# Two-row-block transfers for half-height output weights, a V half in five pieces, and a ring of 14 units between layers in a two-layer decode block

## The chip, the cores and the metric

The kernel runs on one core of one Trainium2 chip. The metric is device time in microseconds (us) of one launch, here the time of one core. TensorE (PE) multiplies matrices, VectorE (DVE), ScalarE (ACT) and GpSimd (POOL) do the element-wise work, and the queue of SyncE (SP) issues nearly all transfers from HBM to on-chip memory. Sixteen DMA engines carry them out.

## The reference

Four blocks follow each other on two rows `x` of 512 numbers (batch 2, one token): attention, feed-forward, attention, feed-forward, each with a layer norm in front and added to `x`.

```python
def _A_ref(x, k_cache, v_cache, wq, wo):       # 32 query heads, 8 KV heads, 32768 cached tokens, Dh 128
    q = (x @ wq).reshape(B, Sq, Hq, Dh).transpose(0, 2, 1, 3)
    k = jnp.repeat(k_cache, 4, axis=1); v = jnp.repeat(v_cache, 4, axis=1)
    p = _softmax(jnp.einsum("bhqd,bhkd->bhqk", q, k) * (Dh ** -0.5), axis=-1)
    o = jnp.einsum("bhqk,bhkd->bhqd", p, v)
    return o.transpose(0, 2, 1, 3).reshape(B, Sq, Hq * Dh) @ wo
def _B_ref(x, w_gate, w_up, w_down):           # 512 -> 1792 -> 512
    return (_gelu(x @ w_gate) * (x @ w_up)) @ w_down
x = x + _A_ref(_layernorm(x), ...); x = x + _B_ref(_layernorm(x), ...)
x = x + _A_ref(_layernorm(x), ...); x = x + _B_ref(_layernorm(x), ...)
```

Both layers read the same caches and weights. All is float32.

## The kernel before, in words

Everything streamed lies in one tile `M` of 110 *units*. A unit is 128 partitions by 512 numbers, 2 KB a partition and 0.262 MB in all. Units 0 to 31, 32 to 63 and 64 to 95 are the slots A, B and C. A head (KV head g, batch row b) needs four slot loads: K in two halves and V in two halves of 32 units each. The slots are used in turn. Units 96 to 107 are a zone of three places of four units (`PL = [96, 100, 104]`), for output weights while heads run and for the smaller matrices between the layers. Units 106 to 109 also hold the softmax's probabilities and its transposes.

All transfers stand in one list, `plan`, made by `add`, `chunk`, `stream` and `add_wo` before the program is written. `pump` issues from its head as long as the target units are free. `free(u, n)` marks units free after the instructions that read them and calls `pump`. The order of transfers is thus fixed, and each waits in SP's queue for the readers of its units. Eight completion semaphores (`DMAHW0` to `DMAHW7` in the listings) are handed out in rotation, so a transfer also waits for the one that stands eight before it.

Output weights: for KV head g, four units (`wo`), multiplied in `project` after the second batch row of g. For g = 3 all four, and for g = 5 two of them, are kept in half height instead (`WIDE = {3: 4, 5: 2}`, array `wl`): each unit becomes two of 64 partitions. `pump` brings them in by eight transfers of eight rows, every fourth row of a block of 32:

```python
for r in (0, 32):
    for j in range(4):
        nc.sync.dma_start(mem(u, n)[r + j:r + 32:4], src[r + j:r + 32:4])
```

That is 1 MB for g = 3 and 0.5 MB for g = 5, in each layer.

A head: `scores` (64 unit products, L304), `softmax`, `values` (64 unit products, L348), `combine`, and after the second batch row `project`. A feed-forward: `center` (mean and residual, L257 to L268), `products` (gate and up weights `gu`, 28 units, L403), `gelu`, `hidden`, `down` (`wd`, 14 units, L446). At the start of an attention layer `center`, then 32 units of `wq` (`query_unit`, L277), `query_copy`, `query_gather`.

Layer 1 walks the heads in reverse, so that its first head is layer 0's last. Of that head 101 of 128 units are kept on chip: all of V, the second half of K (32 units, slot C), and five units of the first half of K, which are copied into free PSUM banks and back. Between the layers `gu`, `wd` and `wq` stream through the three places in turn, four units each. Layer 0's last V half comes in pieces of 24, 4 and 4 units, as does layer 1's. In layer 1's feed-forward `gu` and `wd` go to the slots C and A, `wd` in pieces of 8, 2, 2, 1 and 1; the last `wd` unit is multiplied in another form (L466) after the sum `W` has been copied out.

A copy of a whole bank is made in two halves, `halves` and `scaled`, by ACT and by DVE, and `center` sums its row in two halves as well.

Of the kernel before, what the change touches and what calls it, by code (L numbers as in the profile page):

```python
# [11 lines left out]
F32 = mybir.dt.float32  # L12
# [23 lines left out]
PL = [96, 100, 104]  # L36
# [8 lines left out]
KFREE = CH - NPS  # L45

# [26 lines left out]
def block_kernel(ctx: ExitStack, tc: tile.TileContext, x, consts, kt, vt, wq, wo, wl, gu, wd, out):  # L73
# [13 lines left out]
    sm = cp.tile([P, 24], F32, name="sm")  # L87
# [4 lines left out]
    linv, sq2, rs, var = sm[:, 6:10], sm[:, 10:12], sm[:, 12:14], sm[:, 14:15]  # L92
    rstd, junk, nscale, half, ones = sm[:, 15:16], sm[:, 16:20], sm[:, 20:21], sm[:, 21:22], sm[:, 22:23]
# [11 lines left out]
    def pump():  # L105
        while plan:
# [7 lines left out]
            if src.shape[0] == P:  # L114
                nc.sync.dma_start(mem(u, n), src)
            else:
                for r in (0, 32):
                    for j in range(4):
                        nc.sync.dma_start(mem(u, n)[r + j:r + 32:4], src[r + j:r + 32:4])
# [50 lines left out]

    def add_wo(l, g):
# [7 lines left out]
    for l in range(2):  # L179
# [4 lines left out]
        else:  # L184
            ring = [SLOT_A, SLOT_B, SLOT_C]
            g, b = orders[1][0]
            add(("wq7",), cols(wq, 28, 4), PL[1], 4)
            stream("wq", 1, wq, 28, (4,) * 7, [PL[0], PL[2], PL[1], PL[0], PL[2], PL[1], PL[0]])
            where = {}
            lo = 0  # L190
            for n, u in [(4, PL[2])] + [(4, SLOT_C + 4 * i) for i in range(5)] + [(KFREE - 24, PL[0])]:
                key = ("k", 1, g, b, 0, lo)
                add(key, cols(kt[b, g, 0], lo, n), u, n)
                for i in range(n):
                    where[lo + i] = (key, u + i)
                lo += n
            pieces[("k", 1, g, b, 0)] = where
            g, b = orders[1][1]
            chunk("k", 1, g, b, 0, SLOT_C, (12, 20), 20)
# [5 lines left out]
        for i, (g, b, nm_, h) in enumerate(todo):  # L205
# [33 lines left out]
    zero = xw[:, 0, 0:1].to_broadcast([P, U // 2])  # L239
# [11 lines left out]
    def halves(dst, src):  # L251
        nc.scalar.copy(dst[:, :U // 2], src[:, :U // 2])  # L252
        nc.vector.tensor_copy(dst[:, U // 2:], src[:, U // 2:])  # L253

    def center():
        ws = mem(U_PT + 1)
        nc.scalar.activation(ws[:, :U // 2], W[:, :U // 2], AF.Copy, accum_out=rs[:, 0:1])  # L257
# [3 lines left out]
        for j in range(2):  # L261
            nc.tensor.matmul(X[:, :KC * 4], rs[:, j:j + 1].to_broadcast([P, P]), neg, start=False, stop=(j == 1))
# [17 lines left out]
    def scaled(dst, src):  # L280
        nc.scalar.activation(dst[:, :U // 2], src[:, :U // 2], AF.Copy, scale=rstd)
        nc.vector.tensor_scalar(dst[:, U // 2:], src[:, U // 2:], rstd, None, op0=OP.mult)
# [72 lines left out]
    def combine(acc, oT, g, b):  # L355
        md = mem(U_PT)
        halves(md, acc)
# [279 lines left out]
```

## Time and profile before

| | us |
|---|---|
| three runs | 2602.56, 2600.39, 2602.66 (median 2602.56) |
| the profiled execution: time | 2601.85 |
| its span, first to last instruction | 2600.0 |
| PE busy / weight loads / DVE / ACT in it | 1396.8 / 416.4 / 147.7 / 73.2 |
| HBM read | 1102.93 MB, 424 GB/s over the span |
| mean granted TensorE clock | 0.731 |

The busy times are those of the span. A row of the windows' table gives, for a stretch, each engine's busy time with its count of instructions in brackets, then the granted clock of TensorE, the mean busy share of the 16 DMA engines, and GB/s. Packets are put to the stretch in which they start, so a share can read over 1 in a short stretch. In the chain of work and in the timeline a row has the start, the duration, the engine and the line.

### The profile page before, as it was taken

Reading aid. Unit: us, or ns where it says so; the run is one execution under the profiler, and the core shown is the slowest. Engines: PE = TensorE matmul, PEld = TensorE weight load, DVE = VectorE, ACT = ScalarE, POOL = GpSimd, SP = SyncE. Lnnn points to the kernel's source line nnn. Section 1 sums busy time; section 2 is a strip of 40 time slices with the busy share of each in tenths; the row PEclk is TensorE's granted clock in tenths of the full one; section 3 lists DMA queues with packets and bytes.
Section 4 is the critical chain, followed back from the end, with each engine's and each line's share of the span. In section 5 each row is a group of like instructions: output and inputs, shape, how many; then the busy total and the mean of one; then the engine's idle time right before and its main releaser. Section 6 shows DMA issues by size and latency. Waiting matters only on the chain.

```text
span 2600.0 us, 20521 instructions
## 1 busy us (share of the span) xinstructions
PE 1396.8 (54%) x9558; PEld 416.4 (16%) x9558; DVE 147.7 (6%) x437; ACT 73.2 (3%) x196; POOL 3.2 (0%) x12
## 2 busy tenths in 40 slices
PE   4544554554555545555576455455545464554556
PEld 1111111111111111111122111111111111111112
DVE  0000000000000000000011000000000000000001
ACT  0000000000000000000000000000000000000000
POOL 0000000000000000000000000000000000000000
PEclk9777776677767777776788777667777677776677
DMA  9999999999999999999999999999999999999998
GB/s 421 433 434 434 429 432 434 432 436 410 429 429 435 434 397 435 433 429 435 410 340 431 440 432 434 433 395 434 433 427 435 411 435 435 431 433 433 433 430 352
DMA packets 27092, 1104.25 MB, mean 425 GB/s; under 512 B 3456, under 2 KB 3584, under 8 KB 4608
## 3 DMA queue, kind: packets, MB, share of 16 engines
q1 hardware_dynamic: 26720, 1102.86, 98.7%
q8 instruction: 75, 1.23, 0.2%
q10 hardware_dynamic: 288, 0.09, 0.0%
q14 instruction: 9, 0.07, 0.0%
HBM read 1102.93 MB, written 0.00 MB: 424 GB/s over the span
## 4 chain that ended last, share of the span: by engine, by line
DMA 67%; PE 22%; another core or an unknown queue 10%; issue 0%; DVE 0%; SPq 0%; ACT 0%; ACTq 0%; DVEq 0%
DMA M<-in_vt 51%; PE bank L348 14%; DMA M<-in_kt 13%; PE bank L304 5%; DMA M<-in_wd 1%; DMA cst<-in_consts 1%; PE bank L277 1%; PE bank L446 0%; PE bank L384 0%; PE bank L360 0%; DMA M<-in_gu 0%; PE bank L403 0%; DMA M<-in_wq 0%; PE bank L260 0%
## 5 line engine op out<-in xcount | busy, mean ns | idle before, releaser
L304 PE MATMUL bank<-M,qw 128*32 128x512 f32 x4096 | 588.3, 733 | 515.7 <-DMA M<-in_kt 515.7
L348 PE MATMUL bank<-M 128*16 128x512 f32 x4096 | 583.1, 733 | 482.8 <-DMA M<-in_vt 482.8
L304 PEld LDWEIGHTS bank<-M,qw 128*32 128x32 f32 x4096 | 143.1, 131 | 952.0 <-DMA M<-in_kt 564.9
L348 PEld LDWEIGHTS bank<-M 128*16 128x16 f32 x4096 | 137.4, 113 | 901.5 <-issue 901.4
L307 DVE TENSOR_REDUCE sm<-bank 128x1 f32<-128x512 f32 x64 | 44.3, 692 | 1105.6 <-PE bank L304 1105.6
L332 PE MATMUL bank<-cst,M 128*128 128x128 f32 x256 | 51.1, 348 | 90.5 <-ACT M L329 90.3
L329 ACT ACTIVATE M<-bank,sm 128x512 f32<-128x512 f32 x64 | 43.4, 683 | 1284.4 <-DVE sm L324 1284.4
L253 DVE COPY M<-bank 128x256 f32<-128x256 f32 x33 | 14.0, 425 | 1071.5 <-ACT M L252 1071.5
L332 PEld LDWEIGHTS bank<-cst,M 128*128 128x128 f32 x256 | 36.9, 176 | 100.9 <-ACT M L329 100.9
L333 DVE COPY M<-bank 128x512 f32<-128x512 f32 x64 | 43.8, 692 | 62.7 <-PE bank L332 62.7
L360 PE MATMUL bank<-cst,M 128*128 128x4 f32 x224 | 29.5, 255 | 26.7 <-DVE M L253 26.7
L252 ACT COPY M<-bank 128x256 f32<-128x256 f32 x33 | 12.3, 372 | 1120.4 <-PE bank L348 1112.4
L360 PEld LDWEIGHTS bank<-cst,M 128*128 128x128 f32 x224 | 27.1, 191 | 52.4 <-DVE M L253 52.4
L323 PE MATMUL bank<-cst,sm 128*128 128x128 f32 x32 | 10.3, 322 | 35.0 <-DVE sm L322 35.0
L403 PE MATMUL bank<-M,xw 128*32 128x512 f32 x112 | 22.1, 761 | 5.7 <-DMA M<-in_gu 3.3
L337 PEld LDWEIGHTS bank<-cst,sm 128*128 128x128 f32 x128 | 23.1, 253 | 0.0
L384 PE MATMUL bank<-M,oT 128*2 128x512 f32 x104 | 20.7, 806 | 3.0 <-DVE oT L362 3.0
L277 PE MATMUL bank<-M,xw 128*32 128x512 f32 x128 | 20.8, 746 | 1.8 <-DMA M<-in_wq 1.0
L337 PE MATMUL bank<-cst,sm 128*128 128x4 f32 x128 | 21.1, 270 | 0.0
L248 PE MATMUL bank<-cst,xin 128*2 128x128 f32 x40 | 6.0, 300 | 23.3 <-DMA cst<-in_consts 23.3
L446 PE MATMUL bank<-M,hT 128*2 128x512 f32 x54 | 12.2, 859 | 5.6 <-DMA M<-in_wd 3.7
L323 PEld LDWEIGHTS bank<-cst,sm 128*128 128x128 f32 x32 | 4.2, 133 | 64.4 <-DVE sm L322 64.4
(75 smaller groups left out, 179.8 us busy)
## 6 DMA issues: line engine op xcount, KB each, us to landing
M<-in_wo SPq DMA_DIRECT2D x12, 1024.0 KB
M<-in_vt SPq DMA_DIRECT2D x2, 6144.0 KB
M<-in_wq SPq DMA_DIRECT2D x2, 4096.0 KB
M<-in_gu SPq DMA_DIRECT2D x8, 1024.0 KB
M<-in_wq SPq DMA_DIRECT2D x8, 1024.0 KB
M<-in_kt SPq DMA_DIRECT2D x2, 4096.0 KB
M<-in_kt SPq DMA_DIRECT2D x6, 1024.0 KB
M<-in_gu SPq DMA_DIRECT2D x3, 2048.0 KB
```

The costliest lines, as they stand in the source:

```text
L277: nc.tensor.matmul(Q[32 * k:32 * k + 32, :], xw[:, k, XO - 2 * g:XO - 2 * g + 32], mem(u), start=start, stop=stop)
L304: nc.tensor.matmul(S[32 * t:32 * t + 32, :], w[:, 28 - 4 * c:60 - 4 * c], mem(u), start=start, stop=stop)
L307: nc.vector.tensor_reduce(mx[:, h:h + 1], S, axis=AX.X, op=OP.max)
L323: nc.tensor.transpose(X[:, :P], nm.to_broadcast([P, P]), ident)
L329: nc.scalar.activation(p[h], S[h], AF.Exp, bias=bias, scale=SCALE, accum_out=ls[:, h:h + 1])
L332: nc.tensor.transpose(S[h][:, k * P:(k + 1) * P], p[h][:, k * P:(k + 1) * P], ident)
L333: nc.vector.tensor_copy(mem(U_PT + h), S[h])
L337: nc.tensor.matmul(X[:, P:P + REP], ls[:, h:h + 1].to_broadcast([P, P]), mask, start=(h == 0), stop=(h == 1))
L348: nc.tensor.matmul(acc[32 * t:32 * t + 16, :], mem(U_PT + h)[:, k * P + 32 * t + 16 * e:k * P + 32 * t + 16 * e + 16], mem(u), start=(h == ...
L360: nc.tensor.matmul(X[:, :REP], md[:, c * P:(c + 1) * P], sel[:, 4 * c:4 * c + 4], start=(c == 2), stop=(c == 1))
L384: nc.tensor.matmul(W[32 * t:32 * t + NB, :], oT[:, t, :], mem(u + t - nw), start=(t > 0 and first), stop=final)
L403: nc.tensor.matmul(G[v][32 * t:32 * t + 32, :], xw[:, k, XO:XO + 32], mem(un), start=(k == 0), stop=(k == KC - 1))
```

## The change

Four edits, which go together in one file:

1. The half-height weights are stored with rows in another order, and each block of 32 rows comes in one transfer. The eight rows `j` of the old transfer number `j` are now the middle index of a three-dimensional source, with eight as its outermost size.
2. The zone gets a fourth place of two units, 94 and 95, the last two units of slot C, so that the ring between the layers has 14 units. For it only 30 units of K's second half are kept, 99 units in all, and its last two are loaded again (`k1`). The order in the ring is 104, 94, 96, 100, with 4, 2, 4 and 4 units; the first head's scores follow it.
3. The last V half of each layer comes in pieces of 8, 8, 8, 4 and 4 units, and layer 1's `wd` in 4, 4, 2, 2, 1 and 1.
4. `halves` and `scaled` go: ACT alone copies the bank (512 columns), `center` sums with one ACT instruction and one matmul for the mean instead of two, and the layer norm's scale is applied in `query_gather`, from `rstd2` (two columns), rather than in the copy. `feedforward` makes its one-column `rstd` from it by one more DVE instruction.

```diff
-PL = [96, 100, 104]
+PL = [96, 100, 104, 94]
+RING = [2, 3, 0, 1]
+SIZE = [4, 4, 4, 2]
+KC1 = 30
...
                 for r in (0, 32):
-                    for j in range(4):
-                        nc.sync.dma_start(mem(u, n)[r + j:r + 32:4], src[r + j:r + 32:4])
+                    nc.sync.dma_start(mem(u, n)[r:r + 32], src[r:r + 32].rearrange("(j i) c -> i j c", j=4))
...
+    def ring_stream(name, l, src, total, at):
+        cuts, places, n = [], [], 0
+        while n < total:
+            p = RING[at % 4]
+            cuts.append(SIZE[p])
+            places.append(PL[p])
+            n += SIZE[p]
+            at += 1
+        stream(name, l, src, total, cuts, places)
...
-            add(("wq7",), cols(wq, 28, 4), PL[1], 4)
-            stream("wq", 1, wq, 28, (4,) * 7, [PL[0], PL[2], PL[1], PL[0], PL[2], PL[1], PL[0]])
-            for n, u in [(4, PL[2])] + [(4, SLOT_C + 4 * i) for i in range(5)] + [(KFREE - 24, PL[0])]:
...
+            add(("wq7",), cols(wq, 28, 4), PL[2], 4)
+            ring_stream("wq", 1, wq, 28, 1)
+            stream("k0", 1, kt[b, g, 0], KFREE, (2, 6, 4, 4, 4, 4, 3),
+                   [PL[3]] + [SLOT_C + i for i in (0, 6, 10, 14, 18)] + [PL[1] + 1])
+            add(("k1",), cols(kt[b, g, 1], KC1, CH - KC1), PL[2], CH - KC1)
             g, b = orders[1][1]
-            chunk("k", 1, g, b, 0, SLOT_C, (12, 20), 20)
+            chunk("k", 1, g, b, 0, SLOT_C, (10, 22), 22)
...
-            chunk(nm_, l, g, b, h, ring[i % 3], (24, 4, 4) if last else (CH,))
+            chunk(nm_, l, g, b, h, ring[i % 3], (8, 8, 8, 4, 4) if last else (CH,))
...
-            stream("gu", 0, gu, 28, (4,) * 7, [PL[0], PL[2], PL[1], PL[0], PL[2], PL[1], PL[0]])
-            stream("wd", 0, wd, 14, (4, 4, 4, 2), [PL[2], PL[1], PL[0], PL[2]])
+            ring_stream("gu", 0, gu, 28, 0)
+            ring_stream("wd", 0, wd, 14, 0)
...
-            stream("wd", 1, wd, 14, (8, 2, 2, 1, 1), [SLOT_A, SLOT_A + 8, SLOT_A + 10, SLOT_A + 12, SLOT_A + 13])
+            stream("wd", 1, wd, 14, (4, 4, 2, 2, 1, 1), [SLOT_A + i for i in (0, 4, 8, 10, 12, 13)])
...
-        nc.scalar.activation(ws[:, :U // 2], W[:, :U // 2], AF.Copy, accum_out=rs[:, 0:1])
-        nc.vector.tensor_tensor_reduce(ws[:, U // 2:], W[:, U // 2:], zero, 1.0, 0.0, OP.add, OP.add, rs[:, 1:2])
+        nc.scalar.activation(ws, W, AF.Copy, accum_out=rs)
...
-        nc.vector.tensor_tensor_reduce(junk[:, :NB], v, par, 1.0, EPS, OP.mult, OP.add, var)
-        nc.gpsimd.tensor_tensor(rstd, var, half, op=OP.pow)
+        nc.vector.tensor_scalar_add(var, v, EPS)
+        nc.gpsimd.tensor_tensor(rstd2, var, half.to_broadcast([P, NB]), op=OP.pow)
...
     def query_copy(Q, dst):
-        scaled(dst, Q)
+        nc.scalar.copy(dst, Q)
...
-        nc.vector.tensor_copy(qT[:, :, lo:lo + n, :],
-                              G[:, :REP * 2 * n].rearrange("p (r g b) -> p r g b", r=REP, b=NB))
+        nc.vector.tensor_tensor(qT[:, :, lo:lo + n, :],
+                                G[:, :REP * 2 * n].rearrange("p (r g b) -> p r g b", r=REP, b=NB),
+                                rstd2.unsqueeze(1).unsqueeze(1).to_broadcast([P, REP, n, NB]), op=OP.mult)
...
-        halves(md, acc)
+        nc.scalar.copy(md, acc)
...
+    early = [0, 4, 4, 4, 3, 4, 4, KC1]
+    for m in range(8):
+        n = SIZE[RING[(m + 1) % 4]]
+        u = at(where[s][0])
+        for j in range(n):
+            query_unit(X, s // 4, s % 4, u + j, s < 4, s >= 24)
+            s += 1
+        free(u, n)
...
+        for j in range(min(early[m], KC1 - i)):
             score_unit(S1, w, i, k1[i][1], i < 4, i >= CH - 4)
             free(k1[i][1])
             i += 1
...
+    u = at(("k1",))
+    for i in range(KC1, CH):
+        score_unit(S1, w, i, u + i - KC1, False, True)
+        free(u + i - KC1)
+    peak(S1, 1)
     peak(S0, 0)
```

How the change moves instructions is seen on SP's queue at two places. The listings below give each transfer's line, its target and source tile, its shape (partitions by numbers), how often it stands in a row, and in brackets the semaphores that it waits for; `PE_49`, `DVE_49` and `Activation_49` stand for readers of the target units.

The first place is the middle of layer 0, at the output weights of KV head 3. Before, on SP:

```order
L115 DMA M<-in_vt 128x16384 [waits DMAHW5_49,DMAHW2_49,PE_49]
L119 DMA M<-in_wl 8x4096 [waits DVE_49]
L119 DMA M<-in_wl 8x4096 x4
L119 DMA M<-in_wl 8x4096 [waits DMAHW3_49]
L119 DMA M<-in_wl 8x4096 [waits DMAHW4_49]
L119 DMA M<-in_wl 8x4096 [waits DMAHW5_49]
L115 DMA M<-in_vt 128x16384 [waits DMAHW6_49,PE_49]
```

Now, at the same place:

```order
L119 DMA M<-in_vt 128x16384 [waits DMAHW5_49,DMAHW2_49,PE_49]
L122 DMA M<-in_wl 32x1x4096 x2
L119 DMA M<-in_vt 128x16384 [waits DMAHW3_49,PE_49]
L119 DMA M<-in_kt 128x16384 [waits DMAHW4_49,PE_49]
L119 DMA M<-in_kt 128x16384 [waits DMAHW5_49,PE_49]
```

Before, the last three of the eight small transfers wait for the three slot loads ahead of them, the eighth for the V half right in front (`DMAHW5`), and the next V half stands behind it. Now neither small transfer waits, and the V half behind them waits for readers and for a transfer eight places back.

The second place is between the layers, from the last output weights (`wo`) on. Before, on SP:

```order
L115 DMA M<-in_wo 128x2048
L115 DMA M<-in_gu 128x2048
L115 DMA M<-in_gu 128x2048 [waits PE_49]
L115 DMA M<-in_gu 128x2048 [waits DMAHW7_49,DMAHW4_49,PE_49]
L115 DMA M<-in_gu 128x2048 [waits DMAHW5_49,DMAHW0_49,PE_49]
L115 DMA M<-in_gu 128x2048 [waits DMAHW6_49,DMAHW1_49,PE_49]
L115 DMA M<-in_gu 128x2048 [waits DMAHW7_49,DMAHW2_49,PE_49]
L115 DMA M<-in_gu 128x2048 [waits DMAHW3_49,DMAHW0_49,PE_49]
L115 DMA M<-in_wd 128x2048 [waits DMAHW1_49,PE_49]
```

Now, from the same transfer on:

```order
L119 DMA M<-in_wo 128x2048
L119 DMA M<-in_gu 128x2048 [waits DMAHW3_49,PE_49]
L119 DMA M<-in_gu 128x1024 [waits DMAHW4_49]
L119 DMA M<-in_gu 128x2048 [waits DMAHW5_49]
L119 DMA M<-in_gu 128x2048 [waits DMAHW6_49,DMAHW2_49,PE_49]
L119 DMA M<-in_gu 128x2048 [waits DMAHW7_49,DMAHW3_49,PE_49]
L119 DMA M<-in_gu 128x1024 [waits DMAHW4_49,DMAHW0_49,PE_49]
L119 DMA M<-in_gu 128x2048 [waits DMAHW5_49,DMAHW1_49,PE_49]
L119 DMA M<-in_gu 128x2048 [waits DMAHW6_49,PE_49]
L119 DMA M<-in_wd 128x2048 [waits DMAHW7_49,PE_49]
```

Before, two `gu` pieces (8 units) stand ahead of the one that waits for `project` to release the last `wo` (the third); now three pieces of 10 units do, and the fourth waits for it.

More of the change, by code (lines that the diff above doesn't have):

```diff
@@ L460, in feedforward @@
             ws = mem(U_PT + 1)
-            halves(ws, W)
+            nc.scalar.copy(ws, W)
             for n in range(FD - tail, FD):
@@ L501, in block_kernel @@
             k0 = pieces[("k", 0, g, b, 0)]
+            free(SLOT_C + KC1, CH - KC1)
             free(k0[0][1], KFREE)
@@ L551, in block_kernel @@
             i += 1
-        if gg == 5:
-            take(PL[1], 4)
-            for q, (m, dst) in enumerate([(30, PL[1]), (31, PL[1] + 1), (27, PL[1] + 2), (28, PL[1] + 3)]):
-                (nc.scalar.copy if q % 2 else nc.vector.tensor_copy)(mem(dst), bank[psum[m]])
-    peak(S1, 1)
+        if m == 5:
+            take(PL[0], 4)
+            for q, kk in enumerate((30, 31, 27, 28)):
+                (nc.scalar.copy if q % 2 else nc.vector.tensor_copy)(mem(PL[0] + q), bank[psum[kk]])
+        if m == 6:
+            take(PL[1], 1)
+            nc.vector.tensor_copy(mem(PL[1]), bank[psum[29]])
     restart()
@@ L560, in block_kernel @@
     wnext = window(*orders[1][1])
-    take(PL[0] + 3, 1)
-    nc.scalar.copy(mem(PL[0] + 3), bank[psum[29]])
-    S0, A1 = bank[0], bank[1]
-    where = pieces[("k", 1, g, b, 0)]
-    held = {30: PL[1], 31: PL[1] + 1, 27: PL[1] + 2, 28: PL[1] + 3, 29: PL[0] + 3}
+    where = pieces[("k0", 1)]
+    held = {30: PL[0], 31: PL[0] + 1, 27: PL[0] + 2, 28: PL[0] + 3, 29: PL[1]}
     seq = list(range(24)) + [30, 31, 27, 28, 29] + [24, 25, 26]
-    seen, left = {}, {}
-    for i in seq:
-        left[i % 4] = i
+    left = {i % 4: i for i in seq}
+    seen = set()
     for i in seq:
```

49 lines of the change are left out of this document (13 added, 36 removed).

## The prediction

> **What bounds the kernel now.** First the page's slices and the shares of the chain of waits:
>
> ```profile
> GB/s 421 433 434 434 429 432 434 432 436 410 429 429 435 434 397 435 433 429 435 410 340 431 440 432 434 433 395 434 433 427 435 411 435 435 431 433 433 433 430 352
> DMA 67%; PE 22%; another core or an unknown queue 10%; issue 0%; DVE 0%; SPq 0%; ACT 0%; ACTq 0%; DVEq 0%
> ```
>
> Transfers bound it: nearly every slice of 65 us moves 430 to 435 GB/s, whatever PE does. What can be won lies in the slices that fall short: 410, 397, 395 and 411 (numbers 10, 15, 27, 32), 340 in the middle, 352 at the end. So I asked for windows around these (after the last engine's busy time: granted clock, DMA share, GB/s):
>
> ```profile
> 610.00:650.00 40.00, 19.49 (x141) 6.56 (x141) 2.72 (x8) 1.45 (x4) 0.00 (x0) 0.71 0.95 405
> 930.00:970.00 40.00, 18.82 (x141) 6.51 (x141) 2.63 (x8) 1.45 (x4) 0.00 (x0) 0.74 0.90 377
> 1290.00:1400.00 110.00, 88.91 (x609) 29.68 (x605) 14.12 (x52) 8.69 (x23) 1.41 (x3) 0.85 0.93 370
> 1730.00:1770.00 40.00, 18.43 (x137) 6.23 (x129) 2.72 (x8) 1.45 (x4) 0.00 (x0) 0.76 0.90 379
> 2040.00:2080.00 40.00, 15.57 (x93) 5.59 (x97) 2.72 (x8) 1.45 (x4) 0.00 (x0) 0.59 0.92 389
> 2080.00:2540.00 460.00, 243.85 (x1690) 69.67 (x1682) 23.87 (x65) 10.92 (x30) 0.00 (x0) 0.73 1.00 433
> ```
>
> The undisturbed pace is 433 GB/s, so a unit of 0.262 MB takes 0.605 us. A window of length t at r GB/s has lost t x (433 - r) / 433: 2.6, 5.2, 5.0 and 4.1 us at the four short places, 16.9 together, and 16.0 us between the layers.
>
> **Edit 1, the half-height weights.** The four short places are those of `wl`. Their cause stands in SP's waits and its timeline:
>
> ```profile
> SPq L119 <- DMA M<-in_kt: 103.8, 8, 20.3
> SPq L119 <- DMA M<-in_vt: 74.8, 4, 18.7
> 584.66 50.84 SPq L119 DMA_DIRECT2D M<-in_wl  x8
> 635.61 0.37 SPq L115 DMA_DIRECT2D M<-in_vt  x1
> ```
>
> Eight small issues hold SP's queue for 50.84 us: the last three, in each of four places, wait for slot loads that run (12 waits), since the completion semaphores go round by eight. The next V half is issued only at 635.61, after the load ahead has landed, so no slot load is queued behind it. With two transfers the listing shows neither wait; the V half behind them then needs only its slot, which PE releases long before. These stops go, and 24 issues with them; what is late next is the engines themselves. How they run in the stop shows in windows of 1 us, two of the place with 1 MB and four of one with 0.5 MB:
>
> ```profile
> 632.00:633.00 1.00, 0.00 (x0) 0.00 (x0) 0.00 (x0) 0.00 (x0) 0.00 (x0) 0.50 0.43 180
> 633.00:634.00 1.00, 0.00 (x0) 0.00 (x0) 0.00 (x0) 0.00 (x0) 0.00 (x0) 0.50 0.51 213
> 1748.00:1749.00 1.00, 0.00 (x0) 0.00 (x0) 0.00 (x0) 0.00 (x0) 0.00 (x0) 0.50 0.02 8
> 1749.00:1750.00 1.00, 0.00 (x0) 0.00 (x0) 0.00 (x0) 0.00 (x0) 0.00 (x0) 0.50 0.39 94
> 1750.00:1751.00 1.00, 0.00 (x0) 0.00 (x0) 0.30 (x2) 0.00 (x0) 0.00 (x0) 0.50 0.77 229
> 1751.00:1752.00 1.00, 0.07 (x1) 0.07 (x2) 0.00 (x1) 0.90 (x3) 0.00 (x0) 0.50 1.46 446
> ```
>
> At 1 MB about half the rate is left: `wl` goes to eight of the sixteen engines, and these have work through the stop while the others stand. At 0.5 MB all stand for about 1.8 us (0.98 + 0.61 + 0.23). A slot load has landed only when its last engine is done, and the eight have more bytes: 1.57 MB a layer over eight engines of 433 / 16 GB/s is 7.3 us. Low end: only what the eight lose returns, 2 x 1.8 = 3.6 us. High end: with all else equal the other eight end up 14.5 us ahead, half of it idle on the mean, so 16.9 - 7.3 = 9.6 us. I take 5.5, nearer the low end, because the last engine decides.
>
> Whether 32 rows stay on eight engines no row shows, since the old form had eight rows. [...]
>
> **Edits 2 and 3, between the layers.** The chain of waits there, with SP's release of the last place and three windows:
>
> ```profile
> 1288.54 8.85 PE bank L348 x64
> 1297.47 0.38 ACT M L252
> 1300.77 0.48 ACT M L257 x2
> 1303.13 0.89 PE bank L262 x4
> 1304.26 1.94 PE bank L403 x8
> 1309.87 7.06 DMA M<-in_gu
> 1332.20 0.48 ACT M L257 x2
> 1336.31 1.94 PE bank L277 x8
> 1300.77 11.94 SPq L115 DMA_DIRECT2D M<-in_gu  x5
> 1300.00:1305.00 5.00, 3.68 (x24) 2.33 (x20) 0.95 (x7) 0.64 (x3) 0.00 (x0) 0.74 0.64 211
> 1305.00:1310.00 5.00, 4.80 (x26) 1.09 (x18) 0.17 (x2) 0.00 (x0) 0.55 (x1) 0.58 0.56 185
> 1335.00:1340.00 5.00, 4.74 (x23) 1.85 (x23) 0.68 (x7) 0.45 (x2) 0.55 (x1) 0.51 0.74 269
> ```
>
> PE starts on V's last half at 1288.54, when the 24-unit piece has landed; the other eight units land 8 x 0.605 = 4.8 us later, at 1293.4, but PE ends at 1297.39. In pieces of eight it keeps pace (8.85 / 4 = 2.2 us for each, against 4.8 to load one), and after the landing has four units, 8 of 64 instructions: 1.1 us by this row, 1.9 by L403's eight. So values end near 1294.9, 2.5 us earlier. With edit 4 (below, 0.8 us) the last place is released at about 1297.7 rather than 1300.77, and the first `gu` place at 1302.9 rather than 1306.20.
>
> Meanwhile the queue held, behind V, `wo` and two `gu` pieces: 12 units, 7.3 us, spent at 1300.7. Then came one piece, then nothing until 1306.20: the windows lost 2.6 and 2.9 us. Now 14 units last until 1301.9, and the piece released at 1297.7 until 1304.3, when the next can start: up to 1 us is lost, 4.5 are saved. From the last `wd` (1332.2) to the first use of `wq` (1336.31 + 1.94) nothing is released for 6.1 us; the window lost 1.9. A chain 0.8 us shorter and two units more (1.2 us) cover that. Of the other 16.0 - 5.5 - 1.9 = 8.6 us, gaps behind single pieces, a ring that starts full should save most; I say 7.3. Against this stand two units more to load, 1.2 us. Edit 2 and 3 here: 4.5 + 1.9 + 7.3 - 1.2 = 12.5 us. Low end: the ring changes nothing and the chain alone does, 3.3 - 1.2 = 2.1; high end 16.0 - 1.2 = 14.8. I take 12.5, since each of the two gaps is filled by its own account. The first head's two peaks now follow each other, 0.7 us on DVE, behind the last loaded K units; the slot that this releases is wanted only after 32 further units (19 us of loading), which covers it.
>
> **Edit 4, the copies.** ACT's copy of a whole bank is in the trace, and so is the old pair:
>
> ```profile
> 1357.03 0.58 ACT L562 COPY M<-bank 128x512 f32<-128x512 f32 x1
> 2595.34 0.37 ACT L252 COPY M<-bank 128x256 f32<-128x256 f32 x1 [8.03 <-PE bank L446]
> 2595.81 0.42 DVE L253 COPY M<-bank 128x256 f32<-128x256 f32 x1 [4.14 <-ACT M L252]
> ```
>
> The halves ran one after the other, 0.89 us from start to end, since DVE waited for ACT; one copy saves 0.3. `center` saves 0.1 on its sum and half of L262's 0.89 us: 0.8 together, counted above. In the heads the same saving hides behind transfers, as do the added DVE instruction and the scale in the gather.
>
> **The tail.** Here everything after the last transfer counts:
>
> ```profile
> 2588.01 2.49 PE bank L446 x16
> 2590.51 0.97 PE bank L431 x4
> 2591.73 3.57 PE bank L446 x10
> 2590.00:2592.00 2.00, 1.73 (x12) 1.04 (x12) 0.17 (x1) 0.00 (x0) 0.00 (x0) 0.50 0.24 87
> ```
>
> `wd` came eight units at a time, and PE took them from 2588.01. In two pieces, the first four units are done before the second land, so the next stage starts half of 2.49 us earlier, 1.2, and the one copy saves 0.3: 1.5 us. The later small pieces still land until about 2591.5 (87 GB/s in the last window). At the granted clock of 0.50 the ten instructions take 3.57 us; at full clock they might take a third. Ends: 0.5, if the last landing holds PE, and 3.5. The V pieces of layer 1 hide behind `gu` and `wd`.
>
> **Sum.** 5.5 + 12.5 + 1.5 = 19.5 us off the profiled execution's 2601.85 is 2582.4. The median of the runs lies 0.7 above that execution: 2583. The low ends give 3.6 + 2.1 + 0.5 = 6.2 off, the high ends 9.6 + 14.8 + 3.5 = 27.9.
>
> **Rivals.** *The chain, not the ring, binds between the layers.* For it: the chain of waits shows PE, ACT and DVE in a row there. Against: its longest pieces are waits for `gu` (7.06 us). It saves 2.1 instead of 12.5: 2593. Chance 0.13.
>
> *The engines share evenly after all.* For it, other work may lie on the other eight, such as the instruction fetches:
>
> ```profile
> q8 instruction: 75, 1.23, 0.2%
> ```
>
> 0.2% of sixteen engines' 2600 us is 83 us; on eight engines 10.4 each, near the 14.5 of `wl`. All 16.9 would return, so 2583 - 11.4 = 2572. Chance 0.08.
>
> *The 32-row transfers use fewer engines.* This ends on the other side. The form is new, and no row shows it. On n engines `wl` adds 14.5 x (8 / n - 1) us to each: 14.5 for four, 43.5 for two, which is 2627. It decides from n below 3.4, where 19.5 us are eaten. Against it, only the old form's eight. Chance 0.04.
>
> *Smaller pieces cost what they save.* There are eight more transfers at the V halves, the ring and `wd`. A transfer issued to a dry queue costs a start; by the windows from 1748 that is about 2 us until the full rate. If each paid it, 16 us: 2599, no change that can be told. Against it, queued pieces overlap: from 2080 to 2540 one load follows another at 433 GB/s. [...] Chance 0.05.
>
> **Chances.** My forecast, 2583, has 0.70. A measurement of this kernel can tell about 0.2%, 5.2 us. Faster by more: 0.70 + 0.13 + 0.08 = 0.91; within: 0.05; slower: 0.04. A range of 2574 to 2595 holds the forecast with nearly all of its bounds and the first rival.
>
> **What would show it.** Windows at the four `wl` places near 433 GB/s but for half the engines' lead, and no long wait of SP on L122; if it still waits there, edit 1 failed. Between the layers 110 us should move at some 420 GB/s instead of 370; a chain of PE, ACT and DVE with the queue dry would make me wrong. In the tail L446 should stand before the last landing. A rate well under half at the `wl` transfers would show fewer than eight engines.

## The result, and the profile after

| | before | changed | ratio, 95% interval |
|---|---|---|---|
| first measurement, four runs each | 2601.79 us (2600.39 to 2602.66) | 2589.10 us (2585.00 to 2591.62) | 0.9950 [0.9933, 0.9967] |
| again on another chip, nine and five runs | 2600.84 us (2598.51 to 2604.24) | 2589.67 us (2585.22 to 2589.81) | 0.9951 [0.9938, 0.9963] |

The changed kernel is faster by 0.5%, 12.7 us by the medians. The forecast had 2583 and a saving of 19.5. The median lies inside the forecast's range of 2574 to 2595, but that range also holds the first rival's 2593, so the time alone does not choose between the two. The profiled execution took 2590.02 us (span 2588.2).

The page's slices and the shares of the chain of waits, of the changed kernel:

```profile
GB/s 422 436 432 431 430 436 432 432 436 429 432 432 435 434 430 434 431 435 431 395 349 431 440 432 431 435 429 435 436 427 434 434 435 429 432 435 433 431 433 329
DMA 61%; PE 26%; another core or an unknown queue 12%; issue 1%; DVE 0%; ACT 0%; SPq 0%; DVEq 0%; ACTq 0%
```

Slices 10, 15, 27 and 32 (410, 397, 395 and 411 before) read 429, 430, 429 and 434: the four short places are gone. The middle is no better (395 and 349 after 410 and 340), and the last slice is worse, 329 after 352. The windows say the same (granted clock, DMA share and GB/s stand last):

```profile
610.00:650.00 40.00, 20.84 (x141) 6.98 (x141) 2.72 (x8) 1.45 (x4) 0.00 (x0) 0.71 1.03 443
930.00:970.00 40.00, 20.72 (x141) 5.93 (x141) 2.70 (x8) 1.45 (x4) 0.00 (x0) 0.71 1.00 432
1280.00:1390.00 110.00, 88.82 (x581) 28.71 (x577) 12.40 (x45) 9.39 (x22) 1.70 (x3) 0.83 0.91 367
1290.00:1300.00 10.00, 7.70 (x42) 3.65 (x42) 0.68 (x6) 1.44 (x4) 0.00 (x0) 0.65 0.45 167
1730.00:1770.00 40.00, 19.03 (x133) 5.51 (x129) 2.70 (x8) 1.45 (x4) 0.00 (x0) 0.70 1.00 432
2040.00:2080.00 40.00, 19.65 (x137) 6.58 (x129) 2.72 (x8) 1.45 (x4) 0.00 (x0) 0.71 1.01 435
```

Before, the four places of `wl` had 405, 377, 379 and 389. Between the layers, before had this:

```profile
1280.00:1390.00 110.00, 84.19 (x561) 27.53 (x557) 13.53 (x50) 8.32 (x22) 1.41 (x3) 0.83 0.93 367
1290.00:1300.00 10.00, 8.74 (x72) 2.85 (x68) 0.59 (x2) 0.37 (x1) 0.00 (x0) 0.89 0.79 329
1300.00:1310.00 10.00, 8.48 (x46) 3.42 (x38) 1.12 (x9) 0.64 (x3) 0.55 (x1) 0.66 0.60 198
1330.00:1340.00 10.00, 8.59 (x38) 3.67 (x32) 1.12 (x9) 0.92 (x4) 0.55 (x1) 0.50 0.86 297
```

The same 367 over 110 us, and in the ten microseconds around V's landing even less, 167 after 329. SP's timeline at the first `wl` place shows that the queue no longer stops:

```profile
584.88 1.57 SPq L122 DMA_DIRECT2D M<-in_wl  x2
604.39 0.34 SPq L119 DMA_DIRECT2D M<-in_vt  x1
```

1.57 us instead of 50.84, and the V half behind is issued at 604.39 instead of 635.61. The chain of waits between the layers (rows of the engines that carry it):

```profile
1266.29 23.94 DMA M<-in_vt
1290.27 1.10 PE bank L345 x8
1292.03 1.11 PE bank L357 x8
1293.38 1.93 PE bank L381 x8
1295.33 0.70 ACT M L259 x2
1296.08 1.86 PE bank L261 x8
1298.65 1.94 PE bank L400 x8
1304.02 5.93 DMA M<-in_gu
```

V's last piece lands at 1290.23 (before: at about 1293.4), four units are left to multiply, and the first gate products start at 1298.65 rather than 1304.26. From the landing that is 8.4 us, before 10.9. L381 and L261 now run slowly: 1.93 and 1.86 us. The same two steps of the kernel before:

```profile
1299.66 1.08 PE bank L384 x8
1301.77 1.36 PE bank L260 x8
```

**The ledger, from the two profiled executions** (a slice is 65 us): the stops gave back 16.9 us; the two slices between the layers lost (410 + 340 - 395 - 349) x 65 / 433 = 0.9; two more units to load cost 1.2; the last slice lost 23 x 65 / 433 = 3.5. Together 11.3 us; the spans differ by 11.8. So all four stops did come back, and in this execution nothing was won between the layers, where the forecast had put most of the saving. Whether edits 2 to 4 failed there, or edit 1 took back what they won, is what the experiments had to tell.

### The profile page after: what moved, and what is told of

Its sections match the earlier page's. It is cut to its first block, busy times and chain, and to the rows that moved or that the text cites. A ratio compares the mean times of both kernels' runs of the same rounds, so it can differ in the third digit from the quotient of the medians.

```text
span 2588.2 us, 20451 instructions
## 1 busy us (share of the span) xinstructions
PE 1395.0 (54%) x9550; PEld 416.1 (16%) x9550; DVE 131.5 (5%) x394; ACT 81.0 (3%) x195; POOL 3.8 (0%) x12
## 4 chain that ended last, share of the span: by engine, by line
DMA 61%; PE 26%; another core or an unknown queue 12%; issue 1%; DVE 0%; ACT 0%; SPq 0%; DVEq 0%; ACTq 0%
DMA M<-in_vt 48%; PE bank L345 16%; DMA M<-in_kt 12%; PE bank L301 7%; DMA M<-in_wd 1%; PE bank L381 0%; PE bank L375 0%; PE bank L357 0%; PE bank L277 0%; PE bank L400 0%; ACT M L354 0%; PE bank L444 0%; PE bank L329 0%; DMA M<-in_gu 0%
## 5 line engine op out<-in xcount | busy, mean ns | idle before, releaser
L354 ACT COPY M<-bank 128x512 f32<-128x512 f32 x32 | 18.8, 586 | 1144.6 <-PE bank L345 1144.6
L357 PE MATMUL bank<-cst,M 128*128 128x4 f32 x224 | 29.6, 255 | 19.7 <-ACT M L354 19.7
L357 PEld LDWEIGHTS bank<-cst,M 128*128 128x128 f32 x224 | 27.1, 191 | 45.5 <-ACT M L354 45.5
L381 PE MATMUL bank<-M,oT 128*2 128x512 f32 x104 | 18.8, 725 | 3.1 <-DVE oT L359 3.1
```

The source lines that it names most:

```text
L354: nc.scalar.copy(md, acc)
L357: nc.tensor.matmul(X[:, :REP], md[:, c * P:(c + 1) * P], sel[:, 4 * c:4 * c + 4], start=(c == 2), stop=(c == 1))
L381: nc.tensor.matmul(W[32 * t:32 * t + NB, :], oT[:, t, :], mem(u + t - nw), start=(t > 0 and first), stop=final)
```

## Experiments

All ratios are to the kernel before on the same chip (medians 2599.54, 2600.84, 2599.58 and 2598.60 us), with 95% intervals. "Lands" is when the last of the sixteen engines has reported a transfer. The reports are the trace's completion records, sixteen for each full transfer; the *lead* is the time between the first and the last of them.

**The changed kernel again**, as reference for the next ones. 

> The changed kernel, unaltered, as the reference for the three beside it. Expected 0.995 of the kernel before (2587 where that one takes 2599.5), as in its first measurement.

Measured: 0.9951 [0.9938, 0.9963], as above.

**Edit 1 alone**, on the kernel before:

```diff
-                    for j in range(4):
-                        nc.sync.dma_start(mem(u, n)[r + j:r + 32:4], src[r + j:r + 32:4])
+                    nc.sync.dma_start(mem(u, n)[r:r + 32], src[r:r + 32].rearrange("(j i) c -> i j c", j=4))
...
```

> The kernel before with edit 1 alone (each block of 32 half-height rows in one transfer). Theory A, the last engine decides: the half-height bytes go to eight engines, 7.3 us a layer more than the others have, and a load has landed only with its last engine; the stops vanish from the windows (430 to 440 GB/s at all four places) but only about 4 us come back, 2598. Theory B, the mean rate decides: all 16.9 us lost at the four places come back, 2585.

Measured: 2594.47 us, 0.9981 [0.9970, 0.9991], 4.9 us faster: near the 4 of the theory that the last engine decides, and far from the other's 16.9. Windows of this kernel around V's landing (1290.0):

```profile
1280.00:1390.00 110.00, 84.74 (x557) 27.74 (x557) 13.53 (x50) 8.31 (x22) 1.41 (x3) 0.80 0.86 339
1290.00:1300.00 10.00, 7.68 (x70) 3.25 (x62) 1.02 (x4) 0.85 (x3) 0.00 (x0) 0.99 0.21 66
```

66 GB/s after 329, at a DMA share of 0.21: most engines had run out of work (the last transfer issued ahead was reported by its first engine at 1282.3 and by its last at 1297.4), since all that comes behind it waits for places that V's landing releases. By the engines' reports the last V piece came to its first engine at 1274.9 and to its last at 1290.0, 15.1 us apart; in the kernel before, where the stops let the engines come level, 3.9 apart. Over the 110 us the loss is 110 x (367 - 339) / 433 = 7.1 us, in the last slice (332 after 352) 3.0: 16.9 - 7.1 - 3.0 = 6.8, and this run's span is 6.8 us shorter. The gain of the stops is paid back where the queue next runs dry.

**The changed kernel without edit 1** (the diff above, backwards). 

> The changed kernel with edit 1 undone (eight transfers of eight rows again). Theory A: about 4 us slower than the changed kernel, 2593, and the four stops are back. Theory B: 16.9 us slower, 2606, so that the other edits alone would have been a loss.

Measured: 2593.06 us, 0.9979 [0.9971, 0.9988]. So edits 2 to 4 alone are worth 5.5 us [3.1, 7.5], where the forecast had 12.5 + 1.5, and undoing edit 1 costs 7 us, between the two theories' 4 and 16.9 and nearer the first. Edit 1 alone saves 0.0019 of the time, the others alone 0.0021, all together 0.0049: by the times the two parts add up. Its windows, to be held against those of before:

```profile
1280.00:1390.00 110.00, 86.70 (x588) 27.70 (x580) 12.12 (x44) 9.28 (x22) 1.69 (x3) 0.88 0.97 392
1290.00:1300.00 10.00, 6.80 (x36) 2.15 (x32) 0.16 (x1) 0.77 (x2) 0.00 (x0) 0.67 0.86 356
1300.00:1310.00 10.00, 8.23 (x44) 3.69 (x46) 0.84 (x8) 0.67 (x3) 0.69 (x1) 0.65 0.73 247
1330.00:1340.00 10.00, 10.00 (x58) 3.75 (x54) 0.62 (x5) 0.58 (x1) 0.69 (x1) 0.66 0.98 365
```

Here the edits can be read at the lead of the kernel before (4.2 us after 3.9): 392 after 367 is 6.4 us saved of the 16.8 that were lost, less 1.2 for the two units. The gap behind V (1290 to 1310) gave 10 x (356 + 247 - 329 - 198) / 433 = 1.8 us, the one at the first `wq` (1330 to 1340) 1.6, all others 3.0. So both answers hold: in this profile the edits won less than half of what was forecast there (5.2 of 12.5), and in the first profile of the changed kernel edit 1 took about as much away at the same place. These are single profiles; how far they vary is seen below, at the old `wd` pieces.

**One transfer of 64 rows over sixteen engines** instead of two of 32 over eight, in the changed kernel, with the old order of rows:

```diff
-                for r in (0, 32):
-                    nc.sync.dma_start(mem(u, n)[r:r + 32], src[r:r + 32].rearrange("(j i) c -> i j c", j=4))
+                nc.sync.dma_start(mem(u, n)[:H], src)
```

> The changed kernel with the 64 half-height rows in one transfer of 64 rows in the old storage order: the same bytes to the same places, but over sixteen engines. Theory A: the eight engines lose 3.6 us of work a layer, so the last V half of layer 0 lands up to 3.6 us earlier and the end up to 7 us earlier: 2582 to 2585. Theory B: bytes and mean rate are the same, no change against the changed kernel, 2589.

Measured: 2606.74 us, 1.0026 [1.0015, 1.0037], 20 us slower than the changed kernel. Neither theory had that. One of its windows, and the slices of its page:

```profile
930.00:970.00 40.00, 20.81 (x141) 5.94 (x141) 2.70 (x8) 1.45 (x4) 0.00 (x0) 0.70 1.00 392
GB/s 420 433 432 433 434 433 432 432 432 395 434 434 433 433 411 432 431 432 433 398 369 439 433 432 432 432 396 433 434 433 431 374 432 434 432 433 432 433 433 344
```

All engines are busy (1.00) and yet move 392 GB/s; in slices 10, 15, 27 and 32 (395, 411, 396 and 374) 22 us are lost against the changed kernel. All sixteen engines report the transfer, but the trace's packet records show each of its packets of 16 KB taking some 1.24 us at the first place, where the changed kernel's take 0.61: twice as many engines at half the rate. The theory of the eight engines is not refuted by this. V's last piece comes to the last engine 10.1 us after the first, instead of 15.1, and the slices in the middle and the last one move more than in the changed kernel (398, 369 and 344 after 395, 349 and 329, together 5.7 us). In this profile the lead did fall and gave time back, and the slow packets cost more.

**No half-height weights at all**, in the changed kernel:

```diff
-WIDE = {3: 4, 5: 2}
+WIDE = {}
```

> The changed kernel with no half-height weights at all: KV heads 3 and 5 take their output weights as the others do, four units of 128 rows over sixteen engines, so the eight engines no longer carry 1.57 MB a layer more than the others. Theory A (a load has landed when its last engine is done, so the eight's extra bytes stand in the sum in full, 7.3 us a layer by bytes, of which the other eight's own half, 3.6, is owed anyway): 3.6 us less in each layer, 7 us less than the changed kernel, 0.9922 of before (2579 to 2582). Theory B (the half-height weights balance something else that the other eight carry, such as the 75 instruction fetches of about 1.45 us each, six of every eight of them on the other eight): no gain, 0.994 to 0.996. If the half height serves to make the tail or a place free earlier: slower than the changed kernel by 1 to 5 us.

Measured: 2584.43 us, 0.9934 [0.9921, 0.9946], 4.4 us below the changed kernel's 0.9951 by the same chip's runs; the intervals overlap a little, and this one holds both theory A's 0.9922 and part of theory B's range. In the profile the last V piece of layer 0 came 8.0 us apart, instead of 15.1 and 13.6 in the two profiles of the changed kernel, so 5.6 to 7.1 us of the lead were `wl`'s bytes (the forecast had 7.3 a layer).

The other 8 go with the instruction fetches (`q8 instruction` on the page, 74 packets here, 1.06 us each on the mean). From one slot load to the next the reports stay as far apart as they were, but for steps in which one engine falls back, mostly by 1.4 to 1.7 us, about as often as there is a fetch (35 up to 1275 us). At V's last piece eight engines stand 0 to 2.0 us behind the first and eight 6.2 to 8.0. In the changed kernel two are level with the first, eleven are 6.2 to 8.1 behind, one 9.5 and two 15.0 to 15.1, which reads as engines with neither burden, with one of the two, and with both. So theory B's premise, most fetches on the engines without `wl`, fits the reports, but two engines carry both, and the last one decides. No run here took the fetches away.

The last slice goes with the lead in all profiles: 327 to 333 GB/s in the eight kernels whose last transfers came 14 to 16 us apart, 344 at 10, 350 to 352 at 8 to 9, 371 at 3.5; only the kernel before (3.6) stands aside with 352, at a clock of 0.50. The window 1280 to 1390 moved 388 GB/s:

```profile
1280.00:1390.00 110.00, 87.64 (x605) 27.75 (x602) 12.29 (x45) 9.28 (x22) 1.69 (x3) 0.88 0.96 388
```

**The ring of twelve units**: edit 2 taken back, 101 units kept and the old order of the first head's products, in the changed kernel:

```diff
-            ring_stream("gu", 0, gu, 28, 0)
-            ring_stream("wd", 0, wd, 14, 0)
+            stream("gu", 0, gu, 28, (4,) * 7, [PL[0], PL[2], PL[1], PL[0], PL[2], PL[1], PL[0]])
+            stream("wd", 0, wd, 14, (4, 4, 4, 2), [PL[2], PL[1], PL[0], PL[2]])
...
```

> The changed kernel with edit 2 taken back: three places of four units between the layers, 101 units kept, the old order of the first head's products; V's five pieces, the single copies and the two transfers stay. The forecast's reading (the ring of 14 units takes 1.9 + 7.3 us of gaps away and costs 1.2): 8 us slower than the changed kernel, 0.998 of before. Rival (the chain of PE, ACT and DVE sets the gaps, and the ring's two units more only cost their 1.2 us of loading): same or 1 us faster, 0.9945 to 0.995. Between the two, from the changed kernel's trace, where 5.0 us were saved between the layers: 2 to 4 us slower.

**A ring of sixteen units**: the fourth place gets four units, 97 are kept:

```diff
-PL = [96, 100, 104, 94]
+PL = [96, 100, 104, 92]
-SIZE = [4, 4, 4, 2]
-KC1 = 30
+SIZE = [4, 4, 4, 4]
+KC1 = 28
...
```

> The changed kernel with the ring between the layers of four places of four units, 16 units, and 97 units kept instead of 99 (two more units to load, 1.2 us). If what is left of gaps there, about 9 us in the changed kernel's trace, is want of places: 4 to 6 us of it return, net 3 to 5 us faster than the changed kernel, 0.993 to 0.994 of before. Rival (PE, ACT and DVE at the granted clock release the places too late whatever their number): 1.2 us slower, 0.9955.

Measured: twelve units 2590.31 us, 0.9957 [0.9944, 0.9971]; sixteen units 2585.31 us, 0.9941 [0.9928, 0.9953]. One window of each, twelve units first:

```profile
1280.00:1390.00 110.00, 86.08 (x557) 28.19 (x549) 11.54 (x43) 9.57 (x23) 1.69 (x3) 0.81 0.90 357
```

```profile
1280.00:1390.00 110.00, 86.82 (x609) 29.17 (x605) 12.30 (x45) 9.29 (x22) 1.69 (x3) 0.84 0.95 390
```

With fourteen, on the same chip, this was:

```profile
1280.00:1390.00 110.00, 87.98 (x561) 28.99 (x555) 12.40 (x45) 9.38 (x22) 1.69 (x3) 0.81 0.93 369
```

The step from twelve to fourteen saves 12 GB/s, 3.0 us, and costs 1.2: 1.8 net, and 1.6 by the ratios. The step to sixteen saves 21 GB/s, 5.3 us, and costs another 1.2: 4.1 net, and 2.6 by the ratios. Each of these time differences lies within its intervals, and the windows are one profile each; the changed kernel's own differ by more (below, at the old `wd` pieces). So the order twelve, fourteen, sixteen is likely and not shown. The forecast's 8 us for the ring of fourteen is excluded (its 0.998 lies above the interval of the twelve units); the rival that places don't matter lies inside that interval, and just outside that of the sixteen units.

**Both: sixteen units and no half height.** 

> The changed kernel with both: no half-height weights, and the ring of sixteen units with 97 units kept. By their single measurements against the changed kernel (0.9934 and 0.9941 against 0.9951) 4.4 and 2.6 us. Theory A (the engines' unequal load costs at each place where the queue runs dry, the ring takes such places away, and both tell on different parts): 7 us less than the changed kernel, 0.9924 (2580 to 2582). Rival (both take the same idle time between the layers): 4 to 5 us less, 0.9934, and beyond it the ring's two more units are only paid.

Measured: 2582.66 us, 0.9932 [0.9920, 0.9944]: no better than full height alone, as the rival had it, though the interval holds theory A's 0.9924 too.

```profile
1280.00:1390.00 110.00, 86.52 (x601) 28.67 (x601) 12.96 (x46) 9.28 (x22) 1.69 (x3) 0.86 0.96 391
```

391 after 388 (full height alone) and 390 (sixteen units alone): this fits the rival, that less lead and more places fill the same idle time. The two kernels without half height have intervals that end below the changed kernel's 0.9951; 2582.66 against 2599.58 is 16.9 us.

**V's last half in 24, 4 and 4 units again**, in the changed kernel:

```diff
-            chunk(nm_, l, g, b, h, ring[i % 3], (8, 8, 8, 4, 4) if last else (CH,))
+            chunk(nm_, l, g, b, h, ring[i % 3], (24, 4, 4) if last else (CH,))
```

> The changed kernel with the last V half of each layer in pieces of 24, 4 and 4 units again. Theory A, the chain of PE, ACT and DVE binds between the layers: values end 2.5 to 3 us later and nothing makes up for it, 2592. Theory B, the ring of places binds: the three pieces queued behind V cover it, 2589.

Measured: 2590.94 us, 0.9962 [0.9949, 0.9974], some 3 us above the changed kernel, within the intervals, and between its two theories: fewer pieces are no gain. What it shows stands in its chain of waits, to be held against the changed kernel's:

```profile
1285.25 8.86 PE bank L345 x64
1294.77 1.07 PE bank L357 x8
1296.08 1.08 PE bank L381 x8
1297.92 1.05 PE bank L261 x8
1299.48 1.93 PE bank L400 x8
```

PE works 8.86 us without a break, and the chain behind it runs at full clock: L381 1.08 and L261 1.05, after 1.93 and 1.86. V lands at 1290.0 and the gate products start 9.5 us later; five pieces have 8.4. They save 3.0 us of products behind the landing (4.1 to 1.1) and lose 1.9 of them again in L381, L261 and the two mean matmuls: the trace has the granted clock at 0.50 from 1292.9 to 1303.2 in the changed kernel, and at 1.00 from 1288.8 to 1299.1 here. That PE now waits between pieces is what the spare products below bear out, and the profiles agree: the step of L261 took 1.86 or 1.87 us in each of the ten profiles with five pieces and no other work for PE between them, and 1.05, 1.06 and 1.36 in the three with three pieces. Without edit 1 it is worse; PE's timeline there:

```profile
1293.22 1.83 PE L346 MATMUL bank<-M 128*16 128x512 f32 x8 [1.43 <-DMA M<-in_vt]
1295.74 1.87 PE L358 MATMUL bank<-cst,M 128*128 128x4 f32 x8 [0.69 <-ACT M L355]
1297.86 1.89 PE L382 MATMUL bank<-M,oT 128*2 128x512 f32 x8 [0.26 <-DVE oT L360]
1303.13 1.93 PE L401 MATMUL bank<-M,xw 128*32 128x512 f32 x8 [0.26 <-DVE xw L265]
```

Every step is at half rate (the granted clock reads 0.50 in the windows from 1295 to 1305), and the gate products start 10.0 us after V's landing at 1293.2. In the changed kernel the clock changes at 1275.8, 1292.9, 1303.2, 1310.0 and 1313.4 (stretches of 17.1, 10.2, 6.8 and 3.4 us, all multiples of 3.4), and L357 had 1.11 us in one run of the changed kernel and 1.89 in the other. What sets these moments was not shown.

**Spare products to keep the clock up**, in the kernel without half height. A spare product multiplies the identity matrix into unused columns of the bank X:

```diff
+FILL = {8: 12, 16: 12, 24: 3, 28: 7}
...
+    def spare(n):
+        for i in range(n):
+            nc.tensor.matmul(X[:, 448:512], ident, ident[:, :64], start=True, stop=True)
...
+                    if keep and h == 1 and i in FILL:
+                        spare(FILL[i])
```

> The kernel without half-height weights (0.9934 of before) with spare products on PE, whose result nothing reads (128x64, into columns of the bank X that are free there): 12, 12, 3 and 7 of them ahead of the second to fifth piece of layer 0's last V half, and 4 and 5 while ACT copies in the combine and in center behind it. Theory A (PE waits between V's pieces, the granted clock then falls to 0.50, and the chain behind V runs at half rate: there L381 took 1.89 us, L261 1.87 and the first eight of L400 1.94, against 1.04, 1.05 and 1.93 where V came as 24, 4 and 4): with PE kept busy L381 and L261 take 1.05 each, the first product of the gate weights starts 1.7 us earlier after V's landing, and 1 to 2 us come off the time: 0.9927 to 0.993. Rival (the clock is not set by these waits): the rows stay at 1.9, and the spare products delay the chain: 0.9934 to 0.994.

Measured: 2588.52 us, 0.9959 [0.9946, 0.9973], some 6 us slower than without them by the ratios, whose intervals just touch. PE's timeline:

```profile
1288.80 1.77 PE L260 MATMUL bank<-cst 128*128 128x64 f32 x14
1290.51 1.05 PE L353 MATMUL bank<-M 128*16 128x512 f32 x8
1293.69 1.04 PE L390 MATMUL bank<-M,oT 128*2 128x512 f32 x8 [0.26 <-DVE oT L368]
1295.83 1.01 PE L267 MATMUL bank<-cst,M 128*128 128x4 f32 x8
1297.33 1.40 PE L409 MATMUL bank<-M,xw 128*32 128x512 f32 x8 [0.26 <-DVE xw L270]
```

The theory's rows came true: the two steps that had 1.89 and 1.87 take 1.04 and 1.01. Its price did not: the spare products took longer than the waits they were to fill, so the last V piece, landed at 1286.9, was multiplied at 1290.5, and the gate products start 10.4 us after the landing instead of 8.4. That is 2 us. The window 1280 to 1390 reads 375 GB/s after 388, 3.3 of the 4.1 us by which the two profiled executions differ, so the rest is lost between the layers too; what loses it was not found.

**Edit 4 taken back**, copies in halves, in the changed kernel:

```diff
+    def halves(dst, src):
+        nc.scalar.copy(dst[:, :U // 2], src[:, :U // 2])
+        nc.vector.tensor_copy(dst[:, U // 2:], src[:, U // 2:])
...
-        nc.scalar.copy(md, acc)
+        halves(md, acc)
...
```

> The changed kernel with edit 4 taken back: copies of a bank in two halves by ACT and DVE, two sums and two matmuls in center, the scale in the copy. The forecast's reading (0.8 us in the chain that releases places between the layers, 0.3 us in the tail, hidden elsewhere): 1.1 us slower, 0.9955 of before, and the rest of the first head's K lands about 0.8 us later than in the changed kernel. If the chain stands on the path in each of the gaps (after V, at the feed-forward's middle, at the first wq), it is paid three times: 2.5 us, 0.996. If the gaps are made by the places and the engines alone: no change, 0.995.

**Layer 1's `wd` in the old pieces**, in the changed kernel:

```diff
-            stream("wd", 1, wd, 14, (4, 4, 2, 2, 1, 1), [SLOT_A + i for i in (0, 4, 8, 10, 12, 13)])
+            stream("wd", 1, wd, 14, (8, 2, 2, 1, 1), [SLOT_A, SLOT_A + 8, SLOT_A + 10, SLOT_A + 12, SLOT_A + 13])
```

> The changed kernel with layer 1's wd again in pieces of 8, 2, 2, 1 and 1. The forecast's reading: the products of wd begin 1.2 us later, and the end comes 0.5 to 1.2 us later, 0.9955 of before. Rival (the tail hangs on the products of the last gate and up weights, or on the last wd landing, not on the first wd piece): no change, 0.995.

Measured: halves 2588.40 us, 0.9956 [0.9943, 0.9969]; old `wd` pieces 2585.70 us, 0.9949 [0.9935, 0.9964]. Neither differs from 0.9951 by what can be told. With halves the rest of the first head's K lands at 1384.6 against 1384.8 (second profile of the changed kernel), so no delay is seen there either.

Up to layer 1's `wd` the kernel with the old pieces is the changed kernel, instruction for instruction. Its window between the layers is therefore a third sample of it:

```profile
1280.00:1390.00 110.00, 86.95 (x621) 27.60 (x613) 12.28 (x45) 9.30 (x22) 1.69 (x3) 0.91 0.94 385
```

385 after 367 and 369, at a granted clock of 0.91 after 0.83 and 0.81, and with the same lead (15.3 us): 4 to 4.6 us between executions of the same instructions (on three chips; the kernel with halves, on this one's chip, read 368). A difference of that size between two windows of one profile each, as of the rings above, does not tell two kernels apart. The chain of the kernel with the old `wd` pieces at its end:

```profile
2528.88 32.74 DMA M<-in_gu
2561.67 1.97 PE bank L400 x16
2566.65 5.33 PE bank L400 x24
2573.99 1.90 PE bank L444 x16
2576.84 1.88 PE bank L444 x10
```

Here the end hangs on the landing of `gu` and the products behind it, not on the pieces of `wd`. The ten products that took 3.57 us in the kernel before take 1.88 with the same pieces.

## Why the forecast was right in its sign and short in its size

**Edit 1, 5.5 us: right, in part by luck.** The stops vanished, the last engine decided, and 4.9 us came of it alone, 0.9979 - 0.9951 or 7 us on top of the other edits. But 5.5 was a choice between 3.6 and 9.6, and the lead that sets it was 15.1 us, twice the 7.3 of `wl` that the forecast knew. That transfers of 32 rows stay on eight engines, on which this term rests, no row of before shows. The trace of the changed kernel agrees with it: each new transfer has nine completion reports, one 1.1 to 1.2 us after its issue and eight at its landing, as each transfer of eight rows has in the kernel before, where a slot load has sixteen. What the forecast did not say is where the rest is lost: at the two places where all engines must be done before work goes on, 7.1 and 3.0 us in the profile of edit 1 alone.

**Edits 2 and 3 between the layers, 12.5 us: this is the term that was mis-sized.** In the kernel with the stops still in place it measured 6.4 - 1.2 = 5.2 in one profile, and by the times all of edits 2 to 4 gave 5.5 [3.1, 7.5] of the 14 forecast. By its own terms, in that profile:
- First gap, 4.5 forecast, 1.8 measured. "14 units last until 1301.9" was counted from V's last landing. The last of these units did come to the last engine at 1301.8, but to the first at 1297.7: each engine goes on as soon as its own share is done, and the first were 4 us ahead. And the chain took 10.0 us from the landing, not the 7.6 that the forecast's 3.3 us off 10.9 meant: it was priced at durations of full clock, while with the five pieces the clock fell (0.50 from 1295 to 1305).
- Second gap, 1.9 forecast, 1.6 measured: near.
- Other gaps, 7.3 forecast, 3.0 measured. "A ring that starts full should save most" had no row behind it. By one profile each, fourteen units instead of twelve are worth 3.0 us gross in all gaps, which is within what profiles of one kernel differ by.

In the changed kernel the three profiles read 367, 369 and 385 there, where before had 367: the engines' lead took away what these edits won, all of it in two profiles and part of it in the third. That is not an overlap of the two gains. With edit 1 alone the window had 339, so edits 2 to 4 won at least as much beside edit 1 (28 GB/s or more) as without it (25), and the times add up. The forecast's sum fell short because this term was too large and the tail's gave little that can be seen; the runs give no sign that adding its terms was wrong.

**The tail, 1.5 us: its reason is not borne out.** After the last `wd` landing the profiled runs differ by 3.5 us (8.3 and 4.8), but the `wd` pieces gave nothing that can be measured; the clock has a large part, 3.57 us for ten products at a clock of 0.50 against 1.88 at 1.00, a half and not the third that the forecast guessed. In one run of the changed kernel the end hangs on the landing of `wd`'s fourth piece, with six products behind it, in the other on `gu`, as with the old pieces. The chain of the first:

```profile
2556.70 25.45 DMA M<-in_wd
2582.19 1.67 PE bank L444 x6
2583.86 0.98 PE bank L464 x8
```

**Edit 4, 0.8 us: not seen in the times, but seen in the chain.** In the changed kernel the clock (0.50 from 1292.9 to 1303.2) hides it; without the edit nothing was later. Two profiles with three V pieces show it: from the end of V's products to the first gate products 5.4 us with single copies (V in 24, 4 and 4) and 6.6 with halves (edit 1 alone), 1.2 us less. Of these, 0.6 lie in the matmuls for the mean, which ran at a clock of 0.50 with halves and mostly at 1.00 without, so the edit itself is worth between 0.6 and 1.2.

**The rivals.** "The chain, not the ring, binds" is neither confirmed nor excluded: the time lies between its 2593 and the forecast, the chain seems to matter (the one window that moved 16 GB/s or more among profiles of the same instructions had the higher clock), and that places do is likely and not shown. "The engines share evenly" is excluded by edit 1 alone, though its premise fits the reports in part: most instruction fetches seem to fall on engines that carry no `wl`. "Fewer engines" is excluded by the reports (eight at each landing) and the rate at the `wl` places (432 to 443 GB/s), and "smaller pieces cost a start each" by the three coarser pieces of V, which gained nothing (0.9962 after 0.9951).

## What to carry to other kernels

A stop of one queue also let uneven engines come level here (V's last piece 3.9 us from its first engine to its last with the stops, 15.1 without), so its whole loss is not the price of removing it: of 16.9 us 4.9 came back, and 7.1 and 3.0 were lost again at the next places that wait for the last engine. Take the cover of a queue from the first engine's finish, the landing from the last one's (1297.7 and 1301.8 for the last of the fourteen units, without edit 1). Before a window of two kernels is compared, see how far two profiles of one kernel differ in it (367, 369 and 385 GB/s here). And the V half cut in five pieces saved 3.0 us of products behind the landing, but PE then waited between pieces, and the chain behind ran at a clock of 0.50 instead of 1.00, which cost 1.9 of them.

## What was not expected of the hardware

- A transfer into 64 partitions gained nothing by sixteen engines instead of eight: its 16 KB packets took some 1.24 us instead of 0.61, and the run became 20 us slower.
- The engines' lead. 5.6 to 7.1 us of it go with the half-height bytes; 8.0 us are left where all transfers are spread over sixteen. These grow on eight of the engines in steps of mostly 1.4 to 1.7 us, about as many as there are instruction fetches, though 75 fetches take only 0.2% of the engines' time.
- The granted clock moves a chain of small steps by more than the copies or the `wd` pieces: from V's landing to the first gate products it took 8.4 us in one profiled run of the changed kernel, 9.9 in the other, and 7.6 in the kernel that differs only in the `wd` pieces.
